# Converting float64 weights in three word operations instead of four, with the later conversions planned closer together

## The chip, the cores and the metric

The kernel runs on one core of a Trainium2 chip. A core has a matrix engine (TensorE, "PE" in the profile, with its weight loads as "PEld"), a vector engine (VectorE, "DVE"), a scalar engine (ScalarE, "ACT"), a general engine (GpSimd, "POOL"), and SyncE ("SP"), which here issues nearly all DMA transfers. Each engine works through its own queue in order and waits on semaphores for the others. On-chip memory is SBUF; matrix products land in PSUM. The metric is device time in microseconds; the kernel is timed in several runs, and one more execution is recorded by the hardware profiler.

## The reference

Causal-by-block attention over 8 batches and 8 heads (576 positions, 64 dimensions, blocks of 64), and behind it a feed-forward layer on the 4608 x 512 result, with a rational function in its middle:

```
scores = q @ k.T / sqrt(64), masked where block(i) < block(j)
attn   = softmax(scores);  x = attn @ v, heads side by side   # 4608 x 512
h = x @ w_in                                                  # 512 -> 2048
P = a0 + a1*h + a2*h^2 + a3*h^3
Q = 1 + |b0|*|h| + |b1|*h^2
out = (P / (Q + 1e-6)) @ w_out                                # 2048 -> 512
```

q, k and v are float32. [...]

## The kernel before, in words

**Two parts that overlap.** Attention runs over 32 pairs (a batch and two heads), each in 10 steps (five row tiles, two halves); the loop at L699 counts these steps. Within a pair: the raw query and key are transposed on PE and split into two parts (`prep`, L401 to L431, issued for pair p+1 in steps 10p+3 and 10p+5), the scores go to PSUM (L484 to L500), DVE takes the negated row maximum (L507, L511), ACT the exponential (L522), POOL scales by the reciprocal sum (L530 to L534), PE transposes the probabilities (L560) and multiplies with the values (L583, L587 for the first six pairs; L610, L626 later). The result goes to a scratch area in DRAM (`xscr`), from which the feed-forward part (class `Ffn`) reads its x tiles (L187).

**The feed-forward part** runs in two phases: the first 10 of the 16 blocks of 128 hidden columns while attention still runs, the other 6 after it. A unit is two such blocks on 256 tokens (phase 0) or one on 512 (phase 1). Its first product is L204; ACT, POOL and DVE evaluate the rational function (L211 to L253) in SBUF tiles with the tags u, v and s, two buffers each; its second product is L272. Products of float32 quality are made of three products each of numbers split in a high and a low part.

**Weight conversion.** `split_weights` yields 20 conversions for the first phase (called 1 to 20 here; 10 blocks, two conversions of w_in and two of w_out for every two blocks) and 12 for the second. One conversion, `place` at L117, takes a 128 x 512 piece of float64: one load by SP into a tile `st` (L121, tag "os", two buffers), whose low words are w0 and high words w1; then on a tile `wa` (L123, tag "u", the same two buffers that the feed-forward units use for their u)

- L126, ACT: the high word, read as a float32, without its sign;
- L127, DVE: not below the float32 whose bits are 896 x 2^20, which stands for the smallest exponent that a float32 can hold;
- L129, DVE: the bits shifted left by 3 and masked, so that the exponent's lower seven bits land in their float32 place;
- L131, DVE: the low word's top three bits are joined to it;
- L133, DVE: the sign and the top exponent bit of the high word are joined to it;
- L138 and L139 (first phase): ACT rounds the float32 to the high part, POOL subtracts to get the low part. L143 to L146 (second phase): the same by way of scratch memory in DRAM.

**What sets the order.** The program issues conversions and feed-forward work at given attention steps: `WSTEPS` (L694) has the steps of the first 20 conversions, namely 9, 18, 27 and 36 for the first four and `WA + WD * i // 4` with WA = 44 for the rest; the 12 others are spread from step 80 over 150 steps (L701). The feed-forward part begins at step 52 (E0) and issues half a unit's work every four steps at first (`UP` = 25 in a hundred, L708); within a step conversions are issued before it. This order is a priority: the program is then laid out by a planner that simulates the engines' time and lets a later instruction go first on an engine where an earlier one isn't ready. Buffers of one tag are handed out in the same plan.

Of the kernel before, what the change touches and what calls it, by code (L numbers as in the profile page):

```python
# [2 lines left out]

# [6 lines left out]
F32 = mybir.dt.float32  # L10
# [3 lines left out]
AF = mybir.ActivationFunctionType  # L14
ALU = mybir.AluOpType
# [22 lines left out]
TLAG = 6  # L38
W0 = 36
WA = 44  # L40
WD = 4
WB0 = 80
WBN = 150
UP = 25
# [14 lines left out]
MASKS = ((None, None), (0, 0), (0, 1), (1, 0))  # L59
QC = 1.0 + 1e-6  # L60

WMIN = struct.unpack("<f", struct.pack("<I", (1023 - 127) << 20))[0]


@with_exitstack
def attn_ffn_kernel(
# [11 lines left out]
    nc = tc.nc  # L78
# [30 lines left out]
    def weight_tiles(pool, f0, nf, dt):  # L109
        wi = [pool.tile([128, 4, nf * 128], dt, name=f"wi{x}{f0}", tag=f"wi{x}") for x in "hl"]  # L110
        wo = [pool.tile([128, nf, DM], dt, name=f"wo{x}{f0}", tag=f"wo{x}") for x in "hl"]
        return wi + wo

    def split_weights(pool, f0, nf, dt):
        wih, wil, woh, wol = weight_tiles(pool, f0, nf, dt)

        def place(dhi, dlo, src, nm):  # L117

            nd, n = src.shape[1:]
            st = ffn.tile([128, 512, 2], I32, name=f"st{nm}", tag="os")  # L120
            nc.sync.dma_start(out=st.rearrange("p (d f) t -> p d (f t)", d=nd), in_=src.bitcast(I32))  # L121
            w0, w1 = st[:, :, 0], st[:, :, 1]
            at = ffn.tile([128, 512], F32, name=f"wa{nm}", tag="u")  # L123
            ai = at.bitcast(I32)

            nc.scalar.activation(out=at, in_=w1.bitcast(F32), func=AF.Abs)  # L126
            nc.vector.tensor_scalar_max(at, at, WMIN)  # L127

            nc.vector.tensor_scalar(out=ai, in0=ai, scalar1=3, scalar2=0x3FFFFFF8,  # L129
                                    op0=ALU.logical_shift_left, op1=ALU.bitwise_and)  # L130
            nc.vector.scalar_tensor_tensor(out=ai, in0=w0, scalar=29, in1=ai,  # L131
                                           op0=ALU.logical_shift_right, op1=ALU.bitwise_or)
            nc.vector.scalar_tensor_tensor(out=ai, in0=w1, scalar=-0x40000000, in1=ai,  # L133
                                           op0=ALU.bitwise_and, op1=ALU.bitwise_or)

            v3 = lambda x: x.rearrange("p (d f) -> p d f", d=nd)
            if dt is F32R:
                nc.scalar.copy(out=dhi, in_=v3(at))  # L138
                nc.gpsimd.tensor_tensor(out=dlo, in0=v3(at), in1=dhi.bitcast(F32), op=ALU.subtract)  # L139
            else:  # L140
                bt = ffn.tile([128, 512], F32R, name=f"wb{nm}", tag="v")
                pt = ffn.tile([128, 512], F32R, name=f"wp{nm}", tag="s")
                nc.scalar.copy(out=bt, in_=at)  # L143
                nc.gpsimd.tensor_tensor(out=pt, in0=at, in1=bt.bitcast(F32), op=ALU.subtract)
                nc.sync.dma_start(out=dhi, in_=v3(bt).bitcast(F32))
                nc.sync.dma_start(out=dlo, in_=v3(pt).bitcast(F32))  # L146

        def steps():
            for f in range(0, nf, 2):
                cs = slice(f * 128, f * 128 + 256)  # L150
                for d in range(0, 4, 2):
                    src = w_in[d * 128:(d + 2) * 128, (f0 + f) * 128:(f0 + f + 2) * 128]
                    place(wih[:, d:d + 2, cs], wil[:, d:d + 2, cs],
                          src.rearrange("(d p) f -> p d f", p=128), f"i{f0}_{f}_{d}")
                    yield
                for d in range(f, f + 2):
                    place(woh[:, d:d + 1, :], wol[:, d:d + 1, :],
                          w_out[(f0 + d) * 128:(f0 + d + 1) * 128, :].rearrange("(d p) e -> p d e", p=128),
                          f"o{f0}_{d}")
                    yield  # L160

        return (wih, wil, woh, wol), steps()
# [166 lines left out]
    with ExitStack() as actx:  # L329
# [363 lines left out]
        wdone = C0  # L693
        WSTEPS = [0] * C0 + [(W0 * (i + 1)) // 4 for i in range(4 - C0)] + [WA + WD * i // 4 for i in range(NWA - 4)]  # L694

# [23 lines left out]
    for f in range(0, NFB, 2):  # L719
        for i, (d, s) in enumerate(zip(wtsB, wscr)):  # L720
            at = (slice(None), slice(None), slice(f * 128, f * 128 + 256)) if i < 2 else (slice(None), slice(f, f + 2))
# [33 lines left out]
```

## Time and profile before

| what | value |
|---|---|
| median of 3 runs | 1302.56 us (1300.33 to 1307.7) |
| the profiled execution: time, span | 1301.48 us, 1299.6 us |
| mean granted clock of TensorE in it | 0.994 |
| busy in the span: PE, DVE, ACT, POOL | 96%, 71%, 71%, 69% |
| DMA: read from and written to HBM | 98.57 MB, 44.04 MB |

The span is what the profiler saw between the first and the last instruction, a little less than the execution's time. Busy shares are means over stages of different kinds; the prediction reads them by stretches of time. In lines of the chain of waits, the chain is followed back from the last instruction, at each step to what released it.

### The profile page before, as it was taken

The page shows a single profiled execution, that of the slowest core. Times are in us where ns is not written, and L with a number is a line of the kernel's source. Part 1 is how long each engine was busy: PE and PEld are TensorE (multiplying, and loading weights), DVE is VectorE, ACT ScalarE, POOL GpSimd, SP SyncE. Part 2 cuts the span into 40 slices and gives each one's busy share as a digit, 9 for nine tenths or more (in the row PEclk, how much of TensorE's full clock was granted, in tenths as well). Part 3 has the DMA queues.
Part 4 walks back from the last instruction along what each step waited for, and adds up shares of the span by engine and source line. Part 5 has one row for each costly group of instructions (what it writes and reads, how often), then busy time and mean ns, then how long its engine had stood idle before and what let it go on. Part 6 is the DMA issues. An engine that isn't in the chain of part 4 may idle for free.

```text
span 1299.6 us, 22697 instructions
## 1 busy us (share of the span) xinstructions
PE 1252.8 (96%) x7644; PEld 1058.3 (81%) x7644; DVE 923.2 (71%) x1735; ACT 927.8 (71%) x2047; POOL 895.6 (69%) x1041
## 2 busy tenths in 40 slices
PE   6879899999999999999999999999999999999997
PEld 4657788888878888888888888897998888888886
DVE  5896667776887768778667677754656776666765
ACT  5776778877788777878868777876776655555553
POOL 4665668777777778787767676766677666666564
PEclk8999899999999999999999999999999999999999
DMA  6675243544443453543434333247111333443423
GB/s 156 179 203 146 67 138 87 142 114 139 123 114 96 137 151 93 151 114 100 116 82 111 90 84 96 72 145 264 61 49 49 107 105 130 130 130 130 147 81 106
DMA packets 210355, 153.80 MB, mean 118 GB/s; under 512 B 137792, under 2 KB 176704, under 8 KB 210240
## 3 DMA queue, kind: packets, MB, share of 16 engines
q1 hardware_dynamic: 210176, 152.36, 40.3%
q8 instruction: 61, 1.00, 0.3%
q14 instruction: 54, 0.44, 0.1%
q0 software_dynamic: 64, 0.00, 0.0%
HBM read 98.57 MB, written 44.04 MB: 110 GB/s over the span
## 4 chain that ended last, share of the span: by engine, by line
PE 74%; DVE 8%; ACT 7%; POOL 5%; DMA 3%; issue 2%; SPq 2%; POOLq 0%; ACTq 0%; DVEq 0%
PE h L204 28%; PE o L272 27%; PE o L626 5%; PE t L560 4%; PE s L500 3%; PE s L497 2%; ACT p L522 2%; PE tp L410 1%; DVE nm L511 1%; POOL p L534 1%; PE s L484 1%; PE o L587 1%; DMA x<-xscr 1%; POOL u L238 1%; POOL gl L250 1%
## 5 line engine op out<-in xcount | busy, mean ns | idle before, releaser
L204 PE MATMUL h<-x,wih 128*128 128x256 f32 (+1 forms) x1872 | 415.6, 313 | 3.0 <-DMA x<-xscr 2.2
L204 PEld LDWEIGHTS h<-x,wih 128*128 128x128 f32 x1872 | 309.2, 190 | 30.6 <-issue 5.0
L204 PE MATMUL h<-x,wil 128*128 128x256 f32 (+1 forms) x936 | 290.7, 311 | 0.0
L272 PE MATMUL o<-woh,gh 128*128 128x512 f32 x576 | 229.2, 398 | 1.5 <-ACT os L282 1.3
L272 PE MATMUL o<-wol,gh 128*128 128x512 f32 x576 | 226.6, 393 | 0.0
L272 PE MATMUL o<-woh,gl 128*128 128x512 f32 x576 | 214.6, 400 | 2.0 <-POOL gl L250 1.8
L534 POOL TENSOR_SCALAR p<-p,rc 128x128 f32<-128x128 f32 (+4 forms) x288 | 178.7, 632 | 49.9 <-DVE rc L531 44.8
L522 ACT ACTIVATE p<-s,nm 128x288 f32<-128x288 f32 (+4 forms) x320 | 167.6, 532 | 59.1 <-DVE nm L511 54.0
L218 POOL TENSOR_TENSOR u<-v,u 128x512 f32<-128x512 f32 x144 | 187.0, 1299 | 32.2 <-ACT v L214 27.3
L204 PEld LDWEIGHTS h<-x,wil 128*128 128x128 f32 x936 | 178.2, 190 | 9.3
L219 DVE TENSOR_TENSOR s<-s,h 128x512 f32<-128x512 f32 x144 | 98.4, 683 | 118.2 <-ACT s L213 59.4
L238 POOL TENSOR_TENSOR u<-s,u 128x512 f32<-128x512 f32 x90 | 116.4, 1293 | 69.1 <-DVE u L236 54.5
L226 ACT ACTIVATE v<-u,qcb 128x512 f32<-128x512 f32 x144 | 105.0, 729 | 73.4 <-POOL u L218 73.3
L211 ACT ACTIVATE u<-h 128x512 f32<-128x512 f32 x144 | 86.0, 597 | 91.1 <-PE h L204 83.2
L511 DVE TENSOR_REDUCE nm<-s 128x1 f32<-128x128 f32 (+4 forms) x288 | 128.2, 477 | 21.7 <-PE s L500 16.8
L560 PE MATMUL t<-ident,p 128*128 128x128 f32 x800 | 125.1, 279 | 7.8 <-POOL p L534 3.8
L272 PEld LDWEIGHTS o<-woh,gh 128*128 128x128 f32 x576 | 108.3, 188 | 24.3 <-ACT os L282 2.4
L272 PEld LDWEIGHTS o<-woh,gl 128*128 128x128 f32 x576 | 104.4, 188 | 26.0 <-POOL gl L250 4.8
L272 PEld LDWEIGHTS o<-wol,gh 128*128 128x128 f32 x576 | 108.3, 188 | 20.3
L574 DVE TENSOR_TENSOR ptrl<-t,ptrh 128x512 fp32r<-128x512 f32 (+1 forms) x182 | 111.6, 626 | 17.4 <-ACT ptrh L573 16.3
L250 POOL TENSOR_TENSOR gl<-u,v 128x512 fp32r<-128x512 f32 x90 | 119.4, 1326 | 2.9
L560 PEld LDWEIGHTS t<-ident,p 128*128 128x128 f32 x800 | 92.7, 141 | 28.6 <-issue 6.0
(107 smaller groups left out, 2511.3 us busy)
## 6 DMA issues: line engine op xcount, KB each, us to landing
x<-xscr SPq DMA_DIRECT2D x56, 256.0 KB, 3.6
xscr<-xl SPq DMA_DIRECT2D x32, 288.0 KB, 2.3
pscr<-os SPq DMA_DIRECT2D x18, 512.0 KB, 2.8
pt<-pscr SPq DMA_DIRECT2D x36, 256.0 KB, 4.3
out_dram<-os SPq DMA_DIRECT2D x36, 256.0 KB, 3.5
qr<-in_q_dram SPq DMA_DIRECT2D x64, 128.0 KB, 2.6
kr<-in_k_dram SPq DMA_DIRECT2D x64, 128.0 KB, 2.5
sti<-in_moe_w_in_dram SPq DMA_DIRECT2D x16, 512.0 KB, 3.9
```

The costliest lines, as they stand in the source:

```text
L204: nc.tensor.matmul(h[:, j, :], lhsT=w[:, dc, fs], rhs=xs[dc][:, hl, :], start=(dc == 0 and i == 0), stop=(dc == 3 and i == 2))
L218: nc.gpsimd.tensor_tensor(out=ut, in0=vt, in1=ut, op=ALU.mult)
L219: nc.vector.tensor_tensor(out=st, in0=st, in1=hf, op=ALU.mult)
L226: nc.scalar.activation(out=vt, in_=ut, func=AF.Ln, bias=qcb)
L238: nc.gpsimd.tensor_tensor(out=ut, in0=st, in1=ut, op=ALU.subtract)
L250: nc.gpsimd.tensor_tensor(out=gl, in0=ut, in1=vt, op=ALU.mult)
L272: nc.tensor.matmul(self.o[m], lhsT=g[:, j, ms], rhs=w[:, f, :], start=(u == 0 and j == 0 and i == 0), stop=(u == nu - 1 and j == NBU[ph] - ...
L511: nc.vector.reduce_max(out=nm[:, j:j + 1], in_=s[d, j][:, :w], axis=AX.X, negate=True)
L522: nc.scalar.activation(out=dst, in_=s.pop((d, j2))[:, :w], func=AF.Exp, bias=nm[:, n:n + 1], scale=1.0, accum_out=sm[:, j2:j2 + 1])
L534: nc.gpsimd.tensor_scalar(out=x, in0=x, scalar1=rc[:, j2:j2 + 1], scalar2=1.0, op0=ALU.mult, op1=ALU.mult)
L560: nc.tensor.transpose(ps[:, 128 * x:128 * x + 128], src[:, 128 * kb:128 * kb + 128], ident)
L574: nc.vector.tensor_tensor(out=dl, in0=src, in1=dh.bitcast(F32), op=ALU.subtract)
```

## The change

The conversion's ACT step multiplies by 2^-112 as it drops the sign. Read as a float32, the high word's exponent field is the upper eight bits of the float64's eleven, so that multiplication subtracts 112 x 2^23 = 896 x 2^20 from the bits: the difference of the two exponent biases, at the place where the float64 has its exponent. Numbers too small for a float32 fall below what the multiplication can hold. The clamp (L127) is then not needed, nor the mask of L129, and from the high word only the sign is joined in the last step. `WD` goes from 4 to 3, so that conversions 5 to 20 get the steps 44 to 55 instead of 44 to 59.

```
-WD = 4
+WD = 3
...
-WMIN = struct.unpack("<f", struct.pack("<I", (1023 - 127) << 20))[0]
+WSCALE = 2.0 ** -112
...
-            nc.scalar.activation(out=at, in_=w1.bitcast(F32), func=AF.Abs)
-            nc.vector.tensor_scalar_max(at, at, WMIN)
-
-            nc.vector.tensor_scalar(out=ai, in0=ai, scalar1=3, scalar2=0x3FFFFFF8,
-                                    op0=ALU.logical_shift_left, op1=ALU.bitwise_and)
+            nc.scalar.activation(out=at, in_=w1.bitcast(F32), func=AF.Abs, scale=WSCALE)
+
+            nc.vector.tensor_scalar(out=ai, in0=ai, scalar1=3, scalar2=None, op0=ALU.logical_shift_left)
             nc.vector.scalar_tensor_tensor(out=ai, in0=w0, scalar=29, in1=ai,
                                            op0=ALU.logical_shift_right, op1=ALU.bitwise_or)
-            nc.vector.scalar_tensor_tensor(out=ai, in0=w1, scalar=-0x40000000, in1=ai,
+            nc.vector.scalar_tensor_tensor(out=ai, in0=w1, scalar=-0x80000000, in1=ai,
                                            op0=ALU.bitwise_and, op1=ALU.bitwise_or)
```

More of the change, by code (lines that the diff above doesn't have):

```diff
@@ L1 @@
-import struct
 from contextlib import ExitStack
```

## The prediction

> **What bounds the kernel now.** I read the page first, then the busy time by stretches, then the chain of waits, then single engines where the chain leaves the TensorE (PE).
>
> ```profile
> span 1299.6 us, 22697 instructions
> ...
> PE 1252.8 (96%) x7644; PEld 1058.3 (81%) x7644; DVE 923.2 (71%) x1735; ACT 927.8 (71%) x2047; POOL 895.6 (69%) x1041
> ```
>
> In 1299.6 - 1252.8 = 46.8 us of the span PE is not busy. The stretches (start, end and length; then busy us and count of PE, PEld, DVE, ACT, POOL; granted clock; DMA share; GB/s) say where:
>
> ```profile
> 20.00:95.00 75.00, 62.14 (x374) 45.21 (x372) 65.56 (x138) 55.82 (x159) 51.59 (x75) 0.95 0.64 181
> 95.00:150.00 55.00, 48.21 (x287) 37.55 (x287) 39.44 (x81) 36.80 (x96) 34.45 (x48) 0.94 0.40 113
> 150.00:1300.00 1150.00, 1131.33 (x6935) 967.64 (x6935) 808.52 (x1493) 826.25 (x1772) 803.75 (x898) 1.00 0.39 113
> ```
>
> From 150 us on PE is busy for 1131.3 of 1150 us, so nothing that DVE or ACT save there reaches the end except through 18.7 us of small gaps. Between 20 and 150 us PE idles 12.9 + 6.8 = 19.7 us, and DVE is the busiest engine of the first stretch (65.6 of 75 us). All later PE work queues behind this part, so a microsecond saved here is one off the end as long as PE has the same work. This is also where the first 20 of the 32 weight conversions run. The chain of waits passes through their L127 (the clamp that the change drops) six times before 96 us, in pieces (start, us, what) that sum to 0.35 + 0.43 + 0.79 + 0.43 + 0.44 + 0.33 = 2.8 us; the first and the last of the six:
>
> ```profile
> 42.11 0.35 DVE wai L127
> ...
> 95.16 0.33 DVE wao L127
> ```
>
> Through the last four conversions, 17 to 20, it passes in fourteen pieces that sum to 12.7 us; the first and the thirteenth:
>
> ```profile
> 115.04 0.34 DVE wai L127
> ...
> 134.15 1.70 DVE wao L133
> ```
>
> The fourteenth is the cast of conversion 20, which stands in ACT's queue ahead of exponentials and of the polynomial's first step, and waits for that word step:
>
> ```profile
> 135.88 0.62 ACT L138 CAST woh<-wao 128x512 fp32r<-128x512 f32 x1 [1.72 <-DVE wao L133]
> ```
>
> PE meanwhile waits for an exponential (in brackets), its longest such wait after the start-up:
>
> ```profile
> 138.20 1.11 PE L410 MATMUL tp<-ident,qr 128*128 128x128 f32 x4 [3.27 <-ACT p L522]
> ```
>
> After it PE runs at half clock (here PE's busy time alone, then clock, DMA share, GB/s):
>
> ```profile
> 138.00:140.00 2.00, 1.61 (x7) 0.50 0.00 0
> 140.00:142.00 2.00, 2.00 (x10) 0.50 0.58 131
> 142.00:144.00 2.00, 2.00 (x11) 0.50 0.00 0
> ```
>
> So conversion 20 costs 3.3 us of waiting, and 1.61 + 2.00 + 2.00 = 5.6 us of work at half clock would be 2.8 us at full clock: 2.8 us more are lost. Together 6.1 us.
>
> **The change part by part.** *The dropped clamp.* 32 DVE instructions go, half of them this row's (ns: least, median, most); the next rows are the shift and the first two-tensor word step:
>
> ```profile
> L127 DVE TENSOR_SCALAR wai<-wai x16: 412/431/1460, 15.4 to 532.0; 128x512 f32<-128x512 f32 x16
> ...
> L129 DVE TENSOR_SCALAR wai<-wai x16: 411/498/1531, 16.2 to 532.8; 128x512 int32<-128x512 int32 x16
> ...
> L131 DVE SCALAR_TENSOR_TENSOR wai<-sti,wai x16: 671/693/1719, 16.6 to 533.9; 128x512 int32<-128x512 int32 x16
> ```
>
> L127's own busy time in the first two stretches:
>
> ```profile
> 20.00:95.00 75.00, 8.48 (x14) 0.95 0.64 181
> 95.00:150.00 55.00, 3.20 (x5) 0.94 0.40 113
> ```
>
> What it is worth before 95 us lies between nothing (another wait takes each place) and 8.5 us (DVE alone sets that stretch). I take what lay on the chain, 2.8 us, because ACT (55.8 us) and PE (62.1) are nearly as full there and cover the rest; without that cover it is 8.5. The part after 95 us belongs to the moved steps below.
>
> By the Trainium skill, "SBUF — State Buffer", section "Who interferes with whom", VectorE in its two-port mode and GpSimd lock each other out of a shared port for a whole instruction, and whichever starts second waits. The spread of L127 from 412 to 1460 ns agrees, and by that rule a wait for the port passes on to L129 when L127 goes. The one long piece (0.79) would then count only 0.41, the clamp 2.4, and the time would be 1295.7.
>
> *The mask leaves L129, and L133 gets another constant.* L127 (one operation, least 412 ns) and L129 (two, 411 ns) last the same, so one operation fewer costs and saves nothing: 0. The bad bound is that a lone shift runs at L131's 671 ns: 20 x 0.26 = 5.2 us of DVE time before 140 us. L133 does the same two operations: 0.
>
> *ACT multiplies by a power of two.* The nearest rows are L233 (immediate scale, SBUF to SBUF) and L214 (scale and bias read from memory):
>
> ```profile
> L214 ACT ACTIVATE v<-u,bab 128x512 f32<-128x512 f32 x90 | 74.2, 824 | 1.2 <-DMA woh<-wbo 1.1
> ...
> L233 ACT ACTIVATE v<-v 128x512 f32<-128x512 f32 x90 | 57.6, 639 | 1.0
> ```
>
> L126 without a scale takes 0.68 us (its row is below), no less than L233: 0. The bad bound is L214's 0.82: 20 x 0.14 = 2.8 us.
>
> *The later steps.* Conversions 5 to 20 (i = 0 to 15) get step 44 + 3i//4 in place of 44 + i. The trace gives steps a time: the query of pair p+1 is prepared in step 10p + 3, and these are DVE's rows for pairs 5 and 6, steps 43 and 53:
>
> ```profile
> 92.70 0.67 DVE L393 SCALAR_TENSOR_TENSOR q<-tp,q 128x512 fp32r<-128x512 f32 x1
> ...
> 112.83 0.69 DVE L393 SCALAR_TENSOR_TENSOR q<-tp,q 128x512 fp32r<-128x512 f32 x1 [1.68 <-ACT q L390]
> ```
>
> The 16th conversion has its clamp at 95.16 us (row above), at about step 44: the planner lets conversions go ahead of their step when an engine is free, so steps 44 to 55 bind nothing for the first sixteen. Conversions 17 to 20 had steps 56 to 59, and the FFN's first unit is issued in step 55 (25 x (55-52+1) // 100 = 1); its u tile and the conversion's wa tile share two buffers. With the change the four have steps 53, 53, 54, 55, all ahead of that unit (in one step conversions come first). The 17th's words were requested 18 us before ACT took them up, behind the unit's own first step:
>
> ```profile
> 95.82 0.53 SPq L121 DMA_DIRECT2D sti<-in_moe_w_in_dram  x1
> ...
> 112.68 0.60 ACT L211 ACTIVATE u<-h 128x512 f32<-128x512 f32 x1
> ...
> 113.84 0.68 ACT L126 ACTIVATE wai<-sti 128x512 f32<-128x512 f32 x1
> ```
>
> After the change I expect the 17th and 18th from about 100 us and the last two done before about 120. SP, the queue of all loads, issues the loads of 19 and 20 earlier, past the value loads of pair 5 and the FFN's x load. Then no conversion stands in ACT's queue at 135 us, and the 6.1 us of wait and half clock go. What comes back: the four Abs and four casts, 4 x (0.68 + 0.62) = 5.2 us of ACT, lie among pair 5's exponentials, and those behind them wait. ACT is busy 36.8 of 55 us there, so some two thirds should fit into gaps; 30% of 5.2 = 1.6 us is my estimate, between 0 (all under PE's own work) and 5.2.
>
> *The last twelve conversions* keep their steps. L127 is on the chain there in one long piece,
>
> ```profile
> 597.71 1.94 DVE wao L127
> ```
>
> but PE is busy for 98% of that stretch by its row above: 0, at best 1.9.
>
> *Sum.* -2.8 (clamp) - 3.3 (wait) - 2.8 (clock) + 1.6 (given back) = -7.3 us. The profiled execution took 1301.48 us, 1.9 above its span, so it would take 1294.2; the median of the runs shown, 1302.56, is 1.1 above that execution, and from it 1295.3 us.
>
> **The rivals.** *Slower: SP's queue blocks.* A conversion's load waits for one of two st buffers, and everything behind it on SP waits too. The loads of 19 and 20, issued earlier, can stand in front of the store and the load that bring the FFN its first x, which are on the chain, while 17 and 18 still hold the buffers:
>
> ```profile
> 104.03 2.42 DMA xscr<-xl
> 106.50 2.75 DMA x<-xscr
> ```
>
> SP waits for a conversion's last word step 14.1 us in 5 times before 150 us, 6.4 at the longest:
>
> ```profile
> SPq L121 <- DVE wao L133: 14.1, 5, 6.4
> ```
>
> One such wait here delays the first unit by 6.4 us; the wait at 138 us stays or finds another place, and a second half clock of 2.8 us joins it: 9.2 - 2.8 (clamp) = +6.4, 1309.0 us. It decides from a wait of about 3 us on. For it: SP waits this way often. Against it: PE has pair 5's attention to do meanwhile. *No change: the wait only moves.* Conversions 17 to 20 stall ACT at 105 to 118 us as they did at 120 to 138, and another wait takes the clamp's place: between 0 and 4 us gained, about 1300.5. For it: DVE and ACT wait for conversions in many places, and a planner that lets work go ahead may reorder. Here also stands the change that does not do what it says: a shift at 671 ns takes 5.2 of the 7.3 us, 1300.5. *The half clock is not in every execution.* The trace shows it once, behind a wait of 3.3 us. If the timed runs before mostly lack it, 2.8 us cannot be gained: 1298.1. By the Trainium skill, "TensorE: Matmul & The Clock Gate", section "What's actually happening", the clock halves after an idle window of some 3.4 us that runs freely, so that a wait of this length meets it or not; no run here shows that yet. *More: DVE alone sets the stretch to 95 us*, as its 65.6 of 75 us suggest: -8.5 - 6.1 + 1.6 = -13.0, 1289.6 us, and with L127's other 3.2 us 1286.4.
>
> **How the numbers follow.** About 0.5% of the time, 6.5 us, is what a measurement can tell from no change: faster is below 1296.0, slower above 1309.1. The forecast has 0.46 (its own range 1290 to 1299; 0.35 of it below 1296), more 0.12, the missing half clock 0.08, no change 0.22, slower 0.12. Faster: 0.35 + 0.12 = 0.47. Slower: 0.12 (that case's 1309.0 lies on the line; I count all of it). Within 0.5%: 0.11 + 0.08 + 0.22 = 0.41. The range goes from 1286, where all of L127 counts, to 1306, into the slower case, because ACT's bounds (2.8 and 5.2) and a new order of the work around the 18.7 us of later gaps are unknown.
>
> **What would show it.** The clamp: one DVE instruction fewer per conversion, the Abs and the shift at their old medians, and less PE idle between 20 and 95 us than 12.9. The steps: all twenty conversions done by about 120 us, no PE wait of over 2 us and no half clock between 120 and 150. Wrong: the same PE idle before 150 us under other names, or the first FFN matmul late behind an SP wait at L121.

## The result and the profile after

The changed kernel takes 1293.18 us (median of 5 runs, 1292.01 to 1295.02) against 1302.56 us before: a ratio of 0.9926 with a 95% interval of 0.99 to 0.9952, faster by 0.74%. The forecast was 1295.3. The total was met, but by luck: two of its terms were wrong, and their errors happened to cancel.

From the weight conversion on, every line of the changed kernel stands lower by one to three: the shift is L127, the two joins L128 and L130, the Abs L125, the casts L135, and the feed-forward products, three lower, L201 and L269.

First the head of the page after (span, then busy time of each engine):

```profile
span 1291.2 us, 22685 instructions
...
PE 1255.1 (97%) x7644; PEld 1059.5 (82%) x7644; DVE 902.8 (70%) x1703; ACT 926.0 (72%) x2047; POOL 896.7 (69%) x1041
```

The 32 clamps are gone from DVE (1735 to 1703 instructions, 923.2 to 902.8 us). PE is not busy for 1291.2 - 1255.1 = 36.1 us, where it was 46.8. The same stretches as in the prediction say where (start, end and length; busy us and count of PE, PEld, DVE, ACT, POOL; clock; DMA share; GB/s):

```profile
20.00:95.00 75.00, 65.00 (x380) 46.17 (x379) 60.28 (x135) 59.60 (x167) 59.21 (x79) 0.95 0.66 198
95.00:150.00 55.00, 50.45 (x314) 40.09 (x313) 31.48 (x68) 36.10 (x94) 32.81 (x47) 0.97 0.34 92
150.00:1300.00 1150.00, 1127.57 (x6903) 964.72 (x6901) 801.69 (x1477) 822.10 (x1767) 798.88 (x895) 1.00 0.39 113
```

PE's idle time falls from 12.9 to 10.0 us before 95 us, from 6.8 to 4.55 up to 150 us, and, up to the end of each span, from 1149.6 - 1131.33 = 18.3 to 1141.2 - 1127.57 = 13.6 us behind that. The rest, 0.9 us, lies before 20 us. So 4.7 of the 10.7 us come from the small gaps after 150 us. PE's busy time grows by 2.3 us, which leaves the 8.4 us of the span.

The three operations that stayed cost what they did. These are the groups of the conversion's tile after the change (ns: least, median, most; first and last start):

```profile
L125 ACT ACTIVATE wai<-sti x16: 668/704/801, 14.6 to 521.8; 128x512 f32<-128x512 f32 x16
...
L127 DVE TENSOR_SCALAR wai<-wai x16: 406/424/783, 15.4 to 523.2; 128x512 int32<-128x512 int32 x16
```

The Abs with a scale has a median of 0.70 us against the 0.68 us that the prediction read for the Abs without one. The shift with one operation has the same least time (406 ns) as the shift with the mask (411).

The wait that was to go has moved. All twenty conversions of the first phase have had their cast by 109 us (the last one of the first row below starts at 108.3; POOL's subtraction behind it ends at 112.3), and nothing is left of the wait at 135 us. But PE now waits 3.15 us at 100 us. These are the cast group, then one instruction each of ACT, PE and DVE around that wait:

```profile
L135 ACT CAST woh<-wao x10: 617/642/690, 31.0 to 108.3; 128x512 fp32r<-128x512 f32 x10
```

```profile
99.55 0.67 ACT L125 ACTIVATE wao<-sto 128x512 f32<-128x512 f32 x1 [3.52 <-POOL wil L136]
...
101.44 1.64 DVE L130 SCALAR_TENSOR_TENSOR wao<-sto,wao 128x512 int32<-128x512 int32 x1
103.00 0.68 DVE L592 TENSOR_TENSOR xl<-o,xh 128x512 fp32r<-128x512 f32 x1
...
103.73 0.29 PE L494 MATMUL s<-mcol,mrow 64*128 64x64 f32 x1 [3.15 <-DVE xl L592]
```

ACT's Abs waits for POOL to leave the shared buffer, the conversion's three word steps follow on DVE at once, and the attention's L592, for which PE waits, stands in DVE's queue behind them. Half clock follows, as it did before (PE's busy time, clock, DMA share, GB/s):

```profile
102.00:104.00 2.00, 0.27 (x1) 1.00 0.43 157
104.00:106.00 2.00, 1.33 (x11) 0.81 0.83 192
106.00:108.00 2.00, 2.00 (x11) 0.50 0.56 218
```

It is the prediction's mechanism, 35 us earlier. The wait is almost as long, 3.15 us for 3.27. The half clock is shorter: summed over slices of 2 us, the clock stays at half for 3.4 us between 95 and 150 us, where it was 6.8 us before, and costs about 1.6 us in place of 2.8 (PE's busy time in each slice times the part of the clock that is missing).

### The profile page after: what moved, and what is told of

It reads as the page before. It is cut to its first block, busy times and chain, and to the rows that moved or that the text cites. A ratio compares the mean times of both kernels' runs of the same rounds, so it can differ in the third digit from the quotient of the medians.

```text
span 1291.2 us, 22685 instructions
## 1 busy us (share of the span) xinstructions
PE 1255.1 (97%) x7644; PEld 1059.5 (82%) x7644; DVE 902.8 (70%) x1703; ACT 926.0 (72%) x2047; POOL 896.7 (69%) x1041
## 4 chain that ended last, share of the span: by engine, by line
PE 80%; ACT 7%; POOL 5%; DVE 3%; DMA 3%; issue 2%; SPq 0%; POOLq 0%; ACTq 0%; DVEq 0%
PE h L201 30%; PE o L269 28%; PE t L557 5%; PE o L623 5%; PE s L497 4%; PE s L494 3%; POOL p L531 2%; ACT p L519 2%; PE tp L407 2%; PE s L481 1%; DMA sto<-in_moe_w_out_dram 1%; PE o L584 1%; DMA x<-xscr 1%; PE o L607 1%; DMA xt<-xh 1%
## 5 line engine op out<-in xcount | busy, mean ns | idle before, releaser
L201 PE MATMUL h<-x,wih 128*128 128x256 f32 (+1 forms) x1872 | 415.8, 313 | 1.7 <-DMA x<-xscr 0.9
L201 PEld LDWEIGHTS h<-x,wih 128*128 128x128 f32 x1872 | 308.9, 190 | 29.3 <-issue 4.4
L201 PE MATMUL h<-x,wil 128*128 128x256 f32 (+1 forms) x936 | 291.6, 312 | 0.0
L269 PE MATMUL o<-woh,gh 128*128 128x512 f32 x576 | 228.8, 397 | 1.3 <-ACT os L279 1.3
L269 PE MATMUL o<-wol,gh 128*128 128x512 f32 x576 | 227.5, 395 | 0.0
L531 POOL TENSOR_SCALAR p<-p,rc 128x128 f32<-128x128 f32 (+4 forms) x288 | 184.9, 653 | 46.1 <-DVE rc L528 40.9
L269 PE MATMUL o<-woh,gl 128*128 128x512 f32 x576 | 213.7, 400 | 1.6 <-POOL gl L247 1.3
L201 PEld LDWEIGHTS h<-x,wil 128*128 128x128 f32 x936 | 177.9, 190 | 9.8
L235 POOL TENSOR_TENSOR u<-s,u 128x512 f32<-128x512 f32 x90 | 116.2, 1291 | 75.0 <-DVE u L233 63.3
L269 PEld LDWEIGHTS o<-woh,gh 128*128 128x128 f32 x576 | 108.5, 188 | 22.9 <-ACT os L279 1.8
L269 PEld LDWEIGHTS o<-wol,gh 128*128 128x128 f32 x576 | 108.5, 188 | 19.6
L269 PEld LDWEIGHTS o<-woh,gl 128*128 128x128 f32 x576 | 104.2, 189 | 24.1 <-POOL gl L247 3.7
L247 POOL TENSOR_TENSOR gl<-u,v 128x512 fp32r<-128x512 f32 x90 | 118.4, 1315 | 3.1
L570 ACT CAST ptrh<-t 128x512 fp32r<-128x512 f32 (+1 forms) x182 | 95.6, 543 | 29.2 <-PE t L557 28.6
```

What stands on the lines that cost most here:

```text
L201: nc.tensor.matmul(h[:, j, :], lhsT=w[:, dc, fs], rhs=xs[dc][:, hl, :], start=(dc == 0 and i == 0), stop=(dc == 3 and i == 2))
L235: nc.gpsimd.tensor_tensor(out=ut, in0=st, in1=ut, op=ALU.subtract)
L247: nc.gpsimd.tensor_tensor(out=gl, in0=ut, in1=vt, op=ALU.mult)
L269: nc.tensor.matmul(self.o[m], lhsT=g[:, j, ms], rhs=w[:, f, :], start=(u == 0 and j == 0 and i == 0), stop=(u == nu - 1 and j == NBU[ph] - ...
L531: nc.gpsimd.tensor_scalar(out=x, in0=x, scalar1=rc[:, j2:j2 + 1], scalar2=1.0, op0=ALU.mult, op1=ALU.mult)
```

## The experiments

Each ratio is to runs of the kernel before on the same chip, with its 95% interval. "Ahead" and "behind" say whether conversions 17 to 20 have steps before or after the first feed-forward unit, which is issued in step 55. "Plan" is the order that the planner made. Code is cut to the lines that differ, with "..." where lines are left out.

**1. One part at a time.** The three operations with the old steps:

```
-WD = 3
+WD = 4
```

> The new three-operation conversion with the old steps (WD = 4). Theory of the prediction: the clamp alone is worth 2.8 us before 95 us, the late wait of PE near 135 us stays, so a ratio of about 0.998 (1299.8 us against 1302.6). Rival, DVE alone sets the early part: nearly the whole gain, 0.992 to 0.994. Rival, the planner's new order decides: anywhere from 0.995 to 1.005.

Measured: 1316.97 us, 1.0084 (1.0055 to 1.0113). The operations alone make the kernel slower.

The new steps with the four operations:

```
-WD = 4
+WD = 3
```

> The old four-operation conversion with the new steps (WD = 3). Theory of the prediction: the late wait and its half clock go, less what comes back, so -4.5 us, a ratio of about 0.9965. Rival, DVE alone sets the early part: 0.999 to 1.001. After reading the profile of the changed kernel, where a wait of 3.2 us with a half clock stands at 100 to 108 us instead of 135 to 144, I lean to less than the theory: 0.998, with the wait moved rather than gone.

Measured: 1307.8 us, 1.0021 (1.0004 to 1.0039): no gain. The wait for conversion 20 at 138 us is gone. PE's waits of a microsecond or more between 95 and 150 us:

```profile
96.21 5.61 PE L587 MATMUL o<-pt,vz 128*128 128x512 f32 x20 [1.00 <-DVE k L393]
105.73 0.29 PE L497 MATMUL s<-mcol,mrow 64*128 64x64 f32 x1 [1.88 <-DVE xl L595]
```

No wait of over 2 us is left. But the second of these is the wait of the changed kernel in a shorter form: the same PE step waits for the same DVE step (L595 here, L592 there), which stands behind a conversion's steps. And half clock follows it too, again for 3.4 us (PE's busy time, clock, DMA share, GB/s):

```profile
106.00:108.00 2.00, 1.60 (x10) 0.62 0.93 228
108.00:110.00 2.00, 2.00 (x11) 0.52 0.97 348
```

The first unit is late, at 119.3 us where it was 112.7:

```profile
L211 ACT ACTIVATE u<-h x1: 587/587/587, 119.3 to 119.3; 128x512 f32<-128x512 f32 x1
```

The same kernel by stretches (PE's busy time, clock, DMA share, GB/s):

```profile
95.00:150.00 55.00, 50.39 (x300) 0.97 0.42 115
150.00:200.00 50.00, 49.79 (x333) 1.00 0.46 127
200.00:260.00 60.00, 58.80 (x396) 1.00 0.40 109
```

And the kernel before in the two later ones:

```profile
150.00:200.00 50.00, 50.00 (x329) 1.00 0.44 125
200.00:260.00 60.00, 60.00 (x412) 1.00 0.41 111
```

Between 95 and 150 us PE idles 4.6 us instead of 6.8. Between 150 and 260 us, where it never idled before, it now does for 0.2 + 1.2 = 1.4. So most of the 2.2 us is given back by 260 us. Over the whole span PE idles 47.2 us against 46.8, and it is busy for 2.5 us longer (1255.3 against 1252.8) with the same matmuls. That the late unit is the cause was not tested.

The two parts do not add up: 1.0084 x 1.0021 would be 1.0105, and together they give 0.9926.

Three operations, steps closer still (conversions 5 to 20 in steps 44 to 51):

```
-WD = 3
+WD = 2
```

> The changed kernel with the later conversions closer still (WD = 2: steps 44 to 51). Conversions 17 to 20 are ahead of the feed-forward part's first unit as with WD = 3, so by the theory that this order is what counts the time is that of the changed kernel, 0.9926 +- 0.001. If the planner's order as such decides, it differs by more than 0.002 in either direction.

Measured: 1294.33 us, 0.9919 (0.9895 to 0.9942), as the change itself.

The kernel before, with the first four conversions one step earlier each, which alters nothing of the change:

```
-W0 = 36
+W0 = 35
```

> The kernel before with the first four conversions' steps at 8, 17, 26 and 35 instead of 9, 18, 27 and 36 (W0 = 35). No instruction is added or removed. It measures what a redrawn plan alone does. The prediction's theory has no gain or loss for it: 0.9985 to 1.0015. If the plan's order as such decides, it moves by 0.002 or more.

Measured: 1305.68 us, 1.0005 (0.9986 to 1.0024). A small nudge to the planner is not worth half a per cent by itself.

**2. DVE's time with the plan held fixed.** Here the program is planned first, and then single instructions are exchanged, so that the order on every engine stays. With the plan of before, each clamp runs on 8 of its 512 columns (the other 504 are not clamped):

```
+            if getattr(i, 'op0', None) == ALU.max and i.outs and getattr(i.outs[0], 'memref', '').startswith('wa'):
+                o = _copy.replace(i.outs[0], ap=[[512, 128], [1, 8]], bass_ap=None)
+                ins[k] = _copy.replace(i, outs=[o], ins=[o, i.ins[1]])
```

> The kernel before with its plan kept to the instruction: after the plan is made, the 32 clamps are cut from 512 columns to 8, so that DVE loses nearly all of their time and nothing is reordered. It leaves out the clamp of 504 of 512 columns. Theory of the prediction, the clamp is worth what lay on the chain: -2.8 us before 95 us and up to -2.3 us in the row of events that ends at 138 us, 0.9961 to 0.9980. Rival, the changed kernel's gain is the new plan's: 0.999 to 1.000. Rival, DVE alone sets the early part: 0.992 or less.

Measured: 1298.26 us, 0.9962 (0.9948 to 0.9975). The cut clamp's group of this run:

```profile
L127 DVE TENSOR_SCALAR wai<-wai x16: 157/172/1209, 15.5 to 527.9; 128x8 f32<-128x8 f32 x16
```

So 0.431 - 0.172 = 0.26 us a conversion are gone, 32 x 0.26 = 8.3 us of DVE's time (all 32 clamps together fall from 20.1 to 11.8 us), and 0.38% of 1302.56 = 4.9 us of the kernel's: 0.6 us for each, or 0.4 to 0.8 by the interval. Its stretches, in the columns of the first table:

```profile
20.00:95.00 75.00, 64.29 (x379) 46.38 (x378) 64.72 (x146) 56.49 (x163) 53.48 (x77) 0.95 0.66 186
95.00:150.00 55.00, 49.45 (x297) 38.72 (x295) 35.64 (x73) 37.30 (x94) 32.01 (x47) 0.94 0.38 106
```

Of the 4.9 us, 2.2 are PE idle time before 95 us (12.9 to 10.7), 1.2 between 95 and 150 us (6.8 to 5.55), and 1.1 from 150 us on (18.3 to 17.1). The wait for conversion 20 is still there:

```profile
134.31 1.11 PE L410 MATMUL tp<-ident,qr 128*128 128x128 f32 x4 [3.03 <-ACT p L522]
```

The opposite: the same plan with each clamp as the form with two tensors.

```
+                ins[k] = _copy.replace(i, op1=ALU.max, is_scalar_tensor_tensor=True, ins=[i.ins[0], i.ins[1], i.ins[0]])
```

> The kernel before with its plan kept: the 32 clamps become two-tensor instructions on the same data (0.67 us in place of 0.41 at least), 0.26 us more of DVE each, nothing reordered. Theory of the prediction, half of what lies before 140 us counts (20 x 0.26 = 5.2 us): 1.001 to 1.003. If DVE alone sets the early part: 1.004. If DVE's time there does not matter: 1.000.

Measured: 1309.01 us, 1.0038 (1.0023 to 1.0053). Its group, 694 ns in the median:

```profile
L127 DVE SCALAR_TENSOR_TENSOR wai<-wai x16: 679/694/1724, 15.4 to 538.2; 128x512 f32<-128x512 f32 x16
```

0.26 us more costs what 0.26 us less saves. But the two profiles show it in different places. With the cut, PE idles less (42.0 us for 46.8) and is busy for as long (1253.0 us for 1252.8). With the longer clamp PE idles about as much (47.5 us), and is busy for 6.5 us longer, at a mean clock of 0.989 against 0.994: by slices of 2 us, work at half clock loses 12.3 us against 6.0. Other executions of the kernel before have clocks from 0.984 to 0.994, so how much of this the longer clamp brings about is not shown.

The plan of the changed kernel, with its shift in the same slower form (joined with zero):

```
+                ins[k] = _copy.replace(i, op1=ALU.bitwise_or, is_scalar_tensor_tensor=True, ins=[*i.ins, z])
```

> The changed kernel with its plan kept: the 32 shifts become two-tensor instructions (joined with a zero), 0.26 us more of DVE each, nothing reordered. If DVE time in the conversions makes the difference, it gives back a part of the gain: 0.9926 + 0.002 to 0.004, so 0.9946 to 0.9966. If the new plan makes the difference: 0.9926 to 0.9935.

Measured: 1298.61 us, 0.9956 (0.9939 to 0.9973), with a shift of 691 ns in the median where it was 424. It gives back 0.30% of the change's 0.74%, though the intervals of the two ratios overlap, so that this price alone is not clear of nothing. Three tests come to about the same price, 0.3 to 0.4% for 0.26 us in each conversion, in two plans and in both directions.

The three operations with the old steps once more, in another plan:

```
-WD = 3
+WD = 4
...
-W0 = 36
+W0 = 35
```

> The three-operation conversion with the old steps (WD = 4), and the first four steps at 8, 17, 26 and 35 (W0 = 35): another plan for the same work as the kernel that had the ratio 1.0084. If that slow time is a rule of conversions 17 to 20 standing behind the feed-forward part's first unit, it is slow again, 1.006 to 1.010. If it is an accident of one plan, it lands elsewhere, 0.995 to 1.003.

Measured: 1316.96 us, 1.0101 (1.0076 to 1.0127). The loss of the operations alone was not the accident of one plan.

**3. Spacing or order.** The new steps do two things: they bring the conversions closer together, and they put conversions 17 to 20 ahead of the first feed-forward unit. Two runs, both with three operations, take these apart. The old spacing, four steps earlier (conversions 17 to 20 in steps 52 to 55):

```
-WA = 44
-WD = 3
+WA = 40
+WD = 4
```

> The changed kernel's three operations with the old spacing of one step (4 quarters), but from step 40 instead of 44, so that conversions 17 to 20 have steps 52 to 55 and stand ahead of the FFN's first unit, as in the changed kernel. If it is the order of these four against the first unit that decides, this is as fast as the changed kernel: 0.9925, about 1293 us. If the closer spacing itself decides (and the order is a by-product), it stays near the three operations with the old steps, 1.008, about 1313 us. In between, 0.996 to 1.003, would mean that both count, or that the later order of the plan decides more than either.

Measured: 1294.1 us, 0.9921 (0.9905 to 0.9937). And the new spacing, three steps later (steps 56, 56, 57, 58):

```
-WA = 44
+WA = 47
```

> The changed kernel with its close spacing (3 quarters of a step) but from step 47, so that conversions 17 to 20 have steps 56, 56, 57 and 58, behind the FFN's first unit as in the kernel before. If the order against the first unit decides: slow, as the three operations with the old steps were, about 1.008. If the spacing decides: as the changed kernel, 0.9925.

Measured: 1315.48 us, 1.0089 (1.0067 to 1.011). With three operations the time goes with the order, and the spacing does nothing:

| three operations | old spacing | new spacing |
|---|---|---|
| 17 to 20 ahead of the first unit | 0.9921 | 0.9926 |
| behind it | 1.0084 | 1.0089 |

In the four profiles the order is as planned: ACT takes up conversion 20 at 103.6 us and the first unit at 113.5 to 113.8 us in the upper two, and the first unit at 108.0 to 108.2 us, ahead of all four conversions, in the lower two. The runs do not separate this order from the four simply standing earlier: with the gain the last of them has step 51 or 55, with the loss 58 or 59, and nothing between was run.

The changed kernel in another plan:

```
-W0 = 36
+W0 = 35
```

> The changed kernel with the first four conversions' spacing one quarter of a step smaller (steps 8, 17, 26, 35 for 9, 18, 27, 36), which changes nothing that the change is about but lets the planner lay out the program again; the same alteration moved the kernel before by 0.05% and the three operations with the old steps by 0.2%. If the gain is a property of the change: 0.990 to 0.995. If the last 0.36% of it is the luck of one plan: 0.996 or more.

Measured: 1293.81 us, 0.9916 (0.9901 to 0.9931). The gain is not the accident of one plan either.

What is slow in the plans with 17 to 20 behind? Not the part that the four conversions are in. This is the run "behind, new spacing" by stretches (PE's busy time, clock, DMA share, GB/s), and below it the changed kernel:

```profile
95.00:150.00 55.00, 50.57 (x306) 0.94 0.35 100
150.00:400.00 250.00, 246.02 (x1674) 1.00 0.43 118
400.00:1000.00 600.00, 581.98 (x3901) 0.99 0.38 108
```

```profile
150.00:400.00 250.00, 248.74 (x1681) 1.00 0.45 122
400.00:1000.00 600.00, 594.41 (x3970) 1.00 0.38 109
```

Between 95 and 150 us PE is busy for about as long in both (50.45 us in the changed kernel, at a clock of 0.97 for 0.94). Between 400 and 1000 us PE idles 18.0 us in the one and 5.6 in the other: 12.4 of the 18.3 us between their spans. PE's waits from 150 to 1000 us name the place (total us, times, longest), first "behind", then the changed kernel:

```profile
PE o L269 <- POOL gl L247: 9.8, 7, 2.5
```

```profile
PE o L269 <- POOL gl L247: 1.3, 2, 0.8
```

L247 is the multiplication on POOL that makes the low part of a feed-forward unit's result, and L269 the second product that reads it. At one of the seven places in "behind", on PE and on POOL:

```profile
433.36 0.94 PE L497 MATMUL s<-k,q 64*128 64x512 f32 x6
436.78 1.22 PE L269 MATMUL o<-woh,gl 128*128 128x512 f32 x2 [2.47 <-POOL gl L247]
```

```profile
432.41 1.43 POOL L630 TENSOR_TENSOR xl<-xl,xt 128x576 fp32r<-128x576 f32 x1 [4.54 <-DVE ptrl L571]
433.79 1.28 POOL L235 TENSOR_TENSOR u<-s,u 128x512 f32<-128x512 f32 x1
435.16 0.21 POOL L527 TENSOR_SCALAR rc<-sm 128x2 f32<-128x2 f32 x1
435.45 1.27 POOL L247 TENSOR_TENSOR gl<-u,v 128x512 fp32r<-128x512 f32 x1
```

The planner has put an attention step (L630) on POOL in front of the unit's two (L235 and L247); it waits 4.54 us, the unit's two wait behind it, and PE starts nothing until they are done. The profile puts the 4.54 us down to DVE, but what L630 reads is xl and xt, and the transfer that fills xt (L627) was issued at 426.53 us and landed 5.7 us later, at 432.2: the wait is more likely for that. At three others of the seven places, near 291, 570 and 881 us, an L630 also runs just before; at the remaining three none does. Why three operations with 17 to 20 behind make the planner choose this, 300 us after the conversions in question, no run shows. With four operations the order behind (the kernel before) has no such loss, so it is not the order alone.

**4. The rest of the table.** Four operations and the new steps, in the plan of the run with the steps alone, and each clamp then cut to 8 columns (504 are not clamped):

```
-WD = 4
+WD = 3
...
+                o = _copy.replace(i.outs[0], ap=[[512, 128], [1, 8]], bass_ap=None)
```

> Four operations and the new steps, planned with the full clamp (the plan of the run with the steps alone), and then each clamp cut to 8 of its 512 columns, as in the run with the old plan. The values of the other 504 columns are not clamped. If the clamp's own DVE time is worth the same 0.4% in any plan, this is 1.0021 - 0.0038 = 0.998, and the rest of the gain to 0.9926 comes from what the planner does when it knows of three operations. If the new steps need the shorter conversion on the chip in order to pay, and not another plan: 0.993.

Measured: 1300.43 us, 0.9974 (0.9961 to 0.9987). The clamp's time is worth 1.0021 - 0.9974 = 0.47% here and 0.38% in the plan of before: about the same. The new steps do not wait for a shorter conversion on the chip in order to pay; they pay nothing by themselves.

No version beats the changed kernel: steps from 40, closer steps and the other first steps lie at 0.9916 to 0.9921, inside its own interval.

## Why the prediction was right in its total and wrong in two terms

**The clamp (-2.8, "what lay on the chain"): mis-sized.** In the stretch for which it was made it looks right: PE's idle time before 95 us fell by 2.9. But that trace has another plan. With the plan held, the cut left 4.83 of L127's 8.48 us between 20 and 95 us, and PE's idle time there fell by 2.2; at that rate of 0.6 the 8.48 us are worth about 5.1 us (an estimate), midway between the 2.8 taken and the upper bound of 8.5. Two places were left out of the sum: the clamps between 95 and 150 us, which the prediction put under the moved steps, and the last twelve, priced at 0 because PE was 98% busy there. With the plan held, the cut gave 1.2 us in the first of these places and 1.1 us from 150 us on. For the whole clamp the same rate gives two estimates. Its working time, 32 x 0.431 = 13.8 us, is worth about 8.2 us. The record has it at 20.1 us; the 6.3 us above the median pieces are waiting, which stayed in the cut clamps (the last section shows for what). If they go with the instruction, it is 11.9 us. The sum of a line's pieces on one chain was too small; the likely reason, not tested by itself, is that a step off that chain becomes the chain once the piece is gone.

**The wait for conversion 20 and its half clock (-3.3 and -2.8): wrong.** The step that failed is "then no conversion stands in ACT's queue at 135 us, and the 6.1 us of wait and half clock go". The first half came true; but a conversion stands in DVE's queue at 101 us instead, and the same pair of costs follows it, 3.15 us and a spell at 0.50. The signs that the prediction named for the steps came true all the same, because they looked at 120 to 150 us only. Between 95 and 150 us the profile does show a part of the gain: 2.2 us less idle time, and a spell at half clock that costs 1.2 us less. The run with the steps alone shows the same two there, 2.2 us and a spell of 3.4 us, and its time did not fall. So this part did not reach the end by itself: the step "a microsecond saved here is one off the end" is the second that failed.

**Given back (+1.6).** No run measures it alone. The first unit starts at 113.8 us in the changed kernel, 1.1 later than before:

```profile
L208 ACT ACTIVATE u<-h x1: 597/597/597, 113.8 to 113.8; 128x512 f32<-128x512 f32 x1
```

**Mask, constant and scale at 0: right,** by the medians above. The bad bound, a shift at 671 ns, was measured as 0.30%, 3.9 us, for all 32; the 5.2 us that it stood at for the first twenty were too much.

**What was not in the sum at all: the plan.** The prediction added up the two edits as if each had its own price. They are not additive: the same three operations are 0.8% slower or 0.8% faster than before, by the order of four conversions against one unit. With the fixed plan's estimates of 8.2 to 11.9 us, or 0.63 to 0.91%, the clamp is worth about the whole of the change's 0.74%; what is left to the plan of the changed kernel is small, and its sign is not known. The slow plans throw the clamp's worth away and lose 0.8% more.

**The rivals.** *SP's queue blocks*: not in the changed kernel, where SP waits for a conversion's last step twice between 95 and 150 us:

```profile
SPq L120 <- DVE wao L130: 1.4, 1, 1.4
SPq L120 <- DVE wai L130: 1.1, 1, 1.1
```

With the steps alone the first unit was 6.6 us late, as this rival had it (6.4); its x load went out at 110.14 us instead of 106.50, behind the loads of conversions 19 and 20. But the time rose by 0.2%, to 1307.8 on that chip, where the kernel before took 1303.96; the rival had +6.4 us. *The wait only moves*: true of the wait, not of the time. *The half clock is not in every execution*: the three profiles with the plan of before (the kernel itself, the clamp cut, the clamp slowed) all have that wait, of 3.03 to 3.27 us; in the cut one, half clock follows (PE's busy time, clock, DMA share, GB/s):

```profile
134.00:136.00 2.00, 1.49 (x7) 0.51 0.00 0
136.00:138.00 2.00, 2.00 (x9) 0.50 0.53 122
138.00:140.00 2.00, 2.00 (x12) 0.50 0.04 10
```

The clocks on record say the same: the profiled execution of the kernel before has a mean clock of 0.994, and its other executions have 0.984 to 0.994. They have more of the slow clock than the profile shows, not less, though not where. This rival falls as far as that can say. *DVE alone sets the stretch*: too much for the clamp before 95 us (8.5, against the estimate of 5.1), and it added the 6.1 us that did not come. *The wait that passes on to L129* (clamp 2.4, 1295.7): with the plan held, the waiting did not pass on; it stayed in the cut clamps, and L129's total went from 21.3 to 20.2 us. What happens to it when the clamp goes altogether, no run with a held plan shows.

## What to carry to other kernels

Where a planner orders the program, price an edit with the order held fixed (exchange the instruction after planning) and apart from that let the whole be planned again: here the first gives an estimated 0.6 to 0.9%, and the second moves the same work by 1.7%. An off-bound engine's time inside a chain of dependent steps is better priced by a rate found from one longer and one shorter form (here 0.6 us for each us of DVE) than by its pieces on the chain of waits. When a cure for a wait works in the trace and the time stays, look for the wait's new place before adding up its gain.

## What was not expected of the hardware

Half clock does not need a wait of 3 us. In the run "behind, new spacing" PE waits 2.37 us for the same POOL step and then runs at half clock until about 914 us (first the matmul with the wait in brackets, then PE's busy time, clock, DMA share, GB/s):

```profile
910.02 0.73 PE L269 MATMUL o<-woh,gl 128*128 128x512 f32 x2 [2.37 <-POOL gl L247]
```

```profile
908.00:910.00 2.00, 0.00 (x0) 1.00 0.00 0
910.00:912.00 2.00, 1.98 (x6) 0.70 0.03 8
912.00:914.00 2.00, 2.00 (x8) 0.50 0.00 0
914.00:916.00 2.00, 2.00 (x18) 0.95 0.00 0
```

Some 3.4 us at half clock lose another 1.7 us, besides the wait itself. The spell of the run with the steps alone, shown above, follows a wait of only 1.88 us. Summed over slices of 2 us, every spell between 16 and 1280 us in the fourteen profiles lasts 3.4 us or twice or three times that. In the run "behind, new spacing" they lose 9.7 us in all, in the changed kernel 5.0; that accounts for PE being busy for longer there with the same matmuls (1259.3 us against 1255.1). The Trainium skill, "TensorE: Matmul & The Clock Gate", section "What's actually happening", puts the slow clock behind an idle window of about 3.4 us that runs freely; the lengths of the spells fit such a window, but the waits of 2.37 and 1.88 us are shorter than it, and the measurement decides.

A DVE step can last as long as a POOL step that runs beside it. A clamp cut to 8 columns takes 0.17 us in the median, yet ten of the 32 take over 0.3 us, and each of the ten ends 0.03 us after a POOL instruction ends. One of them, with the POOL step that had started 0.11 us earlier:

```profile
119.32 1.29 POOL L238 TENSOR_TENSOR u<-s,u 128x512 f32<-128x512 f32 x1 [0.63 <-DVE u L236]
119.43 1.21 DVE L127 TENSOR_SCALAR wai<-wai 128x8 f32<-128x8 f32 x1 [0.19 <-ACT wai L126]
```

In the kernel before, seven of the ten clamps of over 0.6 us end 0.28 us after a POOL instruction in the same way. So the long clamps are waits that the profile counts as busy time, as the prediction's sentence on the shared port has it.
